# Grouped-query decode attention: the tokens of head 6's first values tile, ahead of GpSimd's last wait for the scaled output

## The chip, the core and the metric

One core of a Trainium2 chip runs the kernel. The metric is the device time of one execution in microseconds (us), lower is better. The engines are named as in the profile: PE is TensorE's matrix multiply, PEld its weight load, DVE is VectorE, ACT is ScalarE, POOL is GpSimd, SP is SyncE, which here only issues loads.

## What is computed

One decode step of attention: 32 query heads, one query each, over 8 key and value heads of 65,536 positions with 128 columns, all in bfloat16. Four query heads share one key and value head.

```python
k = jnp.repeat(k, rep, axis=1)          # rep = 32 // 8
v = jnp.repeat(v, rep, axis=1)
scores = jnp.einsum("bhqd,bhkd->bhqk", q, k) * D ** -0.5
p = softmax(scores, axis=-1)
return jnp.einsum("bhqk,bhkd->bhqd", p, v)
```

Keys and values are 268.4 MB together, and each byte is read once.

## The kernel before, in words

**Tiles and ring.** A head's keys and values are each two tiles of 256 rows by 128 partitions (64 KB on a partition, 8.4 MB in all). `buf` holds three of them. SP issues the 32 loads in the order of `tiles` (L153 to L156): from head 2 on `k g 0, k g 1, v g-2 1, v g-1 0`, and last `v 6 1, v 7 0, v 7 1`. Before it reuses a third of `buf`, SP waits until the tile in it has been used (L164, L169). I write v6.0 for the first values tile of head 6, and so on. The last tiles are loaded in pieces with a semaphore for each: v6.0 in 128 and 128 rows, v6.1 in 128, 64, 64, v7.0 in four of 64 (`BY`, L22, semaphores `sL`), and v7.1 in 64, 64, 32, 32, 40, 16 and 8 (`PIECES`, L27, semaphores `sP`).

**Tokens.** PE runs a loop of blocks, not a straight program. The block `values` (L481 to L494) takes one token from the semaphore `sV`, multiplies 32 rows of values by their weights `Ew` (8 matmuls, L486, into `psum_o`) and counts `vit` up by one. A tile of 256 rows is eight tokens. The tokens have no names: whoever counts `sV` up must do so in the order in which PE is to use the rows. For the tiles up to v5.1 SP hands out all eight once the tile has landed (L168). For v6.0 and what follows POOL does it, piece by piece (L216 to L218), `n // 32` tokens for n rows. The last 64 rows of v7.1 have no tokens; the block `tail` (L526) waits for their three pieces itself, the 40 rows at L532 to L538 (L535), the 16 and the 8 at L541 to L548 (L544).

**The round of a head.** PE computes scores of head g in four banks (`bank`, `scores`, L462), then v(g-2).1 in `values`, then `summed` (L502 to L515): it closes `psum_o` (L423), multiplies the maxima (L506), waits for DVE, clears `psum_o` (L420), gathers the result of head g-2 into `psum_f` (L433), and goes on to `values` for v(g-1).0. After that comes `turn` (L516), which takes one count of `wqs`. DVE works in parallel: it transposes the keys (L311) and the weights (L316), masks and sums `psum_o` (L324, L332), makes the maximum ready (L384) and the reciprocal (L338). ACT takes the exponential of the scores (L242), and then scales `psum_f` into `o_out` and counts `outs` up (L249).

**The end.** With the keys of head 7 scored, PE runs v5.1, `summed`, v6.0, `turn`, v6.1, `summed`, v7.0, `turn`, 192 rows of v7.1, and the tail with the last 64 rows, the sum (DVE L324, L332; PE L433), the last scaling (ACT L260) and the store.

**POOL's program around the change.** For g = 1 to 7 POOL waits until `outs` is g and writes the widened queries of head g (L204 to L213). Then it waits until `outs` is 8, counts `wqs` up by two for the two turns that are left (L214), and only then begins the loop that waits for each piece and hands out its tokens. `outs` becomes 8 when ACT has scaled head 5's output, behind the exponential of head 7.

Of the kernel before, what the change touches and what calls it, by code (L numbers as in the profile page):

```python
# [13 lines left out]
G = 8  # L14
# [3 lines left out]
NT = 256  # L18
# [3 lines left out]
BY = {  # L22
    (G - 2, 0): (128, 128), (G - 2, 1): (128, 64, 64), (G - 1, 0): (64, 64, 64, 64),
}
N = 2
STEP = 32
PIECES = (64, 64, 32, 32, 40, 16, 8)  # L27
MOVED = 4
# [3 lines left out]
def kernel(  # L32
# [24 lines left out]
    pe, dve, act, pool, sp = nc.tensor, nc.vector, nc.scalar, nc.gpsimd, nc.sync  # L57
# [38 lines left out]
    def sem(name):  # L96
        sems.append(nc.alloc_semaphore(name))
        return sems[-1]
# [3 lines left out]
    sL = [sem(f"sL{x}") for x in range(sum(map(len, BY.values())))]  # L102
    sP = [sem(f"sP{x}") for x in range(len(PIECES))]
# [5 lines left out]
    vit = sem("vit")  # L109
    scd = sem("scd")  # L110
    vdone = sem("vdone")
    wqs = sem("wqs")
# [7 lines left out]
    outs = sem("outs")  # L120
# [82 lines left out]
    for g in range(G):  # L203
# [7 lines left out]
            in1=quad[:, :].unsqueeze(1).unsqueeze(3).broadcast_to([P, 4, 4, H]),  # L211
            op=ALU.mult,
        ).then_inc(wqs, 1)  # L213
    pool.wait_ge(outs, G).then_inc(wqs, 2)  # L214

    for land, n in list(zip(sL, sum(BY.values(), ()))) + list(zip(sP, PIECES))[:MOVED]:  # L216

        pool.wait_ge(land, 32 if land is sP[0] else 16).then_inc(sV, n // STEP)  # L218

    def take(engine, semaphore, n=1):  # L220

        engine.wait_ge(semaphore, n).then_inc(semaphore, -n)  # L222
# [16 lines left out]
    for g in range(G + 1):  # L239
# [8 lines left out]
        at = max(g - 1, 0) * D  # L248
# [3 lines left out]
        if g == 0:  # L252

            for b in range(3):
                n = sum(kind == "k" and at % 3 == b and 0 < h < G - 1 for at, (kind, h, _) in enumerate(tiles))
# [200 lines left out]
    with block("scores"):  # L456
# [3 lines left out]
        for y in range(4 * N):  # L460
            m, n = y % 4, y // 4
# [64 lines left out]
    with block("tail"):  # L526
        at = sum(PIECES[:MOVED])
# [62 lines left out]
```

## Time and profile before

| what | value |
|---|---|
| runs | 631.0, 632.24, 632.6 us; median 632.24 |
| the profiled execution | 632.93 us |
| its span, first to last instruction | 630.7 us |
| bytes read, over the span | 268.44 MB, 426 GB/s |
| PE busy | 503.5 us, 80% of the span |
| DVE busy | 337.9 us, 54% |
| ACT and POOL busy | 21.1 us and 5.9 us |
| mean granted PE clock | 0.935 of full |

The profiled execution took 2.2 us more than its span; that is time outside the first and last instruction. All positions in time below count from the span's start. A row of the timeline gives the start, the length, engine, line and operation, and in brackets how long the engine had been idle and what ended it. A row of a window gives each engine's busy time in that stretch with its count of instructions, then the mean granted PE clock, the DMA engines' share (1.00 is all 16 busy; it can pass 1 in a short stretch, since a packet's time is put down whole) and the GB/s.

### The profile page before, as it was taken

The numbers are of one execution on the slowest core, as the hardware profiler recorded it, in microseconds if no ns is written. First come the engines' busy times: TensorE is split into PE (matmuls) and PEld (weight loads), VectorE is DVE, ScalarE is ACT, GpSimd is POOL, SyncE is SP. The second block draws the span as 40 slices with busy tenths as digits, with TensorE's granted clock in tenths as the row PEclk, the third lists the DMA queues.
The fourth block names the chain that finished last, engine by engine and source line by source line (L and its number), as shares of the span: only waits on it lengthen the run. The fifth ranks groups of instructions, "written<-read, shape, count | busy, mean of one in ns | idle before, by whom it ended". The sixth has DMA issues, their size and how long they took to land. (4 is left out here: it accounts for less than half of the span.)

```text
span 630.7 us, 8029 instructions
## 1 busy us (share of the span) xinstructions
PE 503.5 (80%) x2189; PEld 204.6 (32%) x2189; DVE 337.9 (54%) x118; ACT 21.1 (3%) x28; POOL 5.9 (1%) x16
## 2 busy tenths in 40 slices
PE   0685398898994979939799398994889987879998
PEld 0232043343331333314333133331333333323333
DVE  3984994789214882158721686217852688210100
ACT  1000100100010000100001000010000100010000
POOL 2000000000000000000000000000000000000000
PEclk9999599798998899988999798997999999898999
DMA  8999999999999999999999999999999999999995
GB/s 368 432 463 403 461 399 466 399 466 399 466 420 445 453 411 461 403 466 399 466 399 466 399 466 399 466 399 466 399 466 399 432 432 466 399 432 431 422 427 217
DMA packets 7000, 268.46 MB, mean 426 GB/s; under 512 B 856, under 2 KB 856, under 8 KB 1112
## 3 DMA queue, kind: packets, MB, share of 16 engines
q1 hardware_dynamic: 6912, 268.44, 98.8%
q10 hardware_dynamic: 88, 0.02, 0.0%
HBM read 268.44 MB, written 0.01 MB: 426 GB/s over the span
## 5 line engine op out<-in xcount | busy, mean ns | idle before, releaser
L311 DVE STREAM_TRANSPOSE buf<-buf 128x8192 f32<-128x8192 f32 x32 | 277.2, 8694 | 84.8 <-DVEq L222 84.8
L462 PE MATMUL sc<-buf,zeros 128*128 x1024 | 244.0, 396 | 0.0
L486 PE MATMUL psum_o<-buf,Ew 128*16 x1008 | 228.1, 385 | 13.6 <-PEq L222 9.7
L462 PEld LDWEIGHTS sc<-buf,zeros 128*128 x1024 | 101.6, 99 | 134.6 <-issue 38.7
L486 PEld LDWEIGHTS psum_o<-buf,Ew 128*16 x1008 | 90.2, 89 | 148.6 <-issue 55.1
L420 PE MATMUL sc<-zeros 128*128 128x512 bf16 x32 | 13.6, 426 | 87.2 <-PEq L222 87.0
L324 DVE TENSOR_TENSOR o_m<-psum_o,pick 128x512 f32<-128x512 f32 x10 | 7.0, 696 | 99.0 <-DVEq L222 72.1
L320 DVE COPY o_r<-o_r 4x1 f32<-4x1 f32 x9 | 1.3, 142 | 76.7 <-DVEq L222 64.1
L420 PEld LDWEIGHTS sc<-zeros 128*128 128x128 bf16 x32 | 3.1, 98 | 96.4 <-issue 95.4
L242 ACT ACTIVATE zeros<-sc,nmb 128x2048 bf16<-128x2048 f32 x8 | 15.7, 1967 | 536.6 <-DVE nmb L384 536.6
L316 DVE STREAM_TRANSPOSE Ew<-zeros 128x1024 bf16<-128x1024 bf16 x18 | 22.3, 1240 | 19.6 <-PE psum_o L486 19.5
L371 DVE TENSOR_REDUCE mx<-sc 128x1 f32<-128x2048 f32 x8 | 18.0, 2252 | 0.0
L506 PE MATMUL misc<-each,same 128*128 128x512 f32 x18 | 10.8, 685 | 8.3 <-PEq L222 8.3
L443 PE MATMUL misc<-qt,rep 32*128 32x128 bf16 x1 | 0.3, 281 | 10.6 <-DVE qt L301 10.6
L420 PE MATMUL psum_o<-zeros 128*128 128x512 bf16 x10 | 4.5, 446 | 5.3 <-PEq L222 5.3
L332 DVE TENSOR_REDUCE o_r<-o_m 128x128 f32<-128x512 f32 x10 | 6.9, 692 | 1.2
L208 POOL TENSOR_TENSOR zeros<-qx,quad 128x64 bf16<-128x64 bf16 x8 | 2.4, 294 | 487.6 <-ACT o_out L249 481.4
L506 PEld LDWEIGHTS misc<-each,same 128*128 128x128 f32 x18 | 2.9, 203 | 8.6 <-issue 8.5
L423 PE MATMUL sc<-zeros 128*128 128x1 bf16 x32 | 5.2, 163 | 0.0
L420 PEld LDWEIGHTS psum_o<-zeros 128*128 128x128 bf16 x10 | 1.0, 98 | 12.8 <-issue 12.6
L287 DVE CAST rep<-ident 32x128 bf16<-32x128 f32 x1 | 2.9, 2877 | 2.7 <-POOL ident L193 2.7
L423 PEld LDWEIGHTS sc<-zeros 128*128 128x128 bf16 x32 | 3.0, 95 | 3.9
(32 smaller groups left out, 37.3 us busy)
## 6 DMA issues: line engine op xcount, KB each, us to landing
buf<-in_k_dram SPq DMA_DIRECT2D x8, 4096.0 KB, 28.4
buf<-in_v_dram SPq DMA_DIRECT2D x8, 2048.0 KB, 34.4
buf<-in_v_dram SPq DMA_DIRECT2D x3, 4096.0 KB, 31.5
buf<-in_v_dram SPq DMA_DIRECT2D x2, 1024.0 KB, 32.7
buf<-in_v_dram SPq DMA_DIRECT2D x1, 1280.0 KB, 36.4
buf<-in_v_dram SPq DMA_DIRECT2D x1, 512.0 KB, 37.2
buf<-in_v_dram SPq DMA_DIRECT2D x1, 256.0 KB, 36.9
buf<-in_k_dram SPq DMA_DIRECT2D x12, 34.6
```

Source lines behind the costliest of these rows:

```text
L242: act.activation(out=E[:, :], in_=sc[:, :], func=ACT.Exp, bias=nmb[:, 0:1], scale=SCALE, accum_out=o_r[:, D:D + 1],).then_inc(exd, 1)
L287: dve.tensor_copy(out=rep[:, :].rearrange("p (a x) -> p a x", a=4), in_=ident[0:32, 0:32].unsqueeze(1).broadcast_to([32, 4, 32]),)
L311: dve.transpose(out=kv, in_=kv).then_inc(kt, 1)
L316: return dve.transpose(out=Ew[:, at], in_=E[:, at])
L324: return dve.tensor_tensor(out=o_m[:, :].rearrange("p (y d) -> p y d", y=4), in0=psum_o[:, :].rearrange("p (y d) -> p y d", y=4), in1=pick ...
L332: return dve.tensor_reduce(out=o_r[:, 0:D], in_=o_m[:, :].rearrange("p (y d) -> p d y", y=4), axis=AX.X, op=ALU.add)
L371: after(dve.tensor_reduce(out=mx[:, :], in_=sc[:, :], axis=AX.X, op=ALU.max))
L420: return pe.matmul(out=bank, lhsT=zer[:, 0:P], rhs=zer[:, :], start=True, stop=False)
L423: return pe.matmul(out=bank[:, 0:1], lhsT=zer[:, 0:P], rhs=zer[:, 0:1], start=False, stop=True)
L462: pe.matmul(out=bank, lhsT=moved(wq[:, m * SLIDE + 4 * n:][:, 0:P], slide), rhs=moved(T[:, n, m // 2, m % 2], keys), start=False, stop=False,)
L486: last = pe.matmul(out=psum_o[0:16, :], lhsT=moved(Ew[:, column(4 * j + 3):][:, 0:16], weight), rhs=moved(buf[:, 4 * j * D:][:, 0:4 * D], ...
L506: pe.matmul(out=misc[:, :], lhsT=same[:, :], rhs=each[:, :].unsqueeze(1).broadcast_to([P, 16, 32]), start=True, stop=True,).then_inc(pes, 1)
```

## The change

POOL's wait for `outs` at 8, with its two counts of `wqs`, moves from ahead of the loop into it: behind the second piece. In its old place stands a wait for `vit` at 96, that is for the last matmul of v5.1. So the two pieces of v6.0 are handed out, four tokens each, once v5.1 has been used and they have landed; then comes the wait for the scaled output, and then the pieces of v6.1, v7.0 and v7.1 as before.

```diff
-    pool.wait_ge(outs, G).then_inc(wqs, 2)
-
-    for land, n in list(zip(sL, sum(BY.values(), ()))) + list(zip(sP, PIECES))[:MOVED]:
+
+    pool.wait_ge(vit, NT // STEP * (2 * G - 4))
+    for at, (land, n) in enumerate(list(zip(sL, sum(BY.values(), ()))) + list(zip(sP, PIECES))[:MOVED]):
 
         pool.wait_ge(land, 32 if land is sP[0] else 16).then_inc(sV, n // STEP)
+        if at == 1:
+            pool.wait_ge(outs, G).then_inc(wqs, 2)
```

No other instruction changes on any engine.

## The prediction

> **What bounds the kernel now.** I read the DMA part of the page first: the loads on SP's queue kept the 16 DMA engines at work for 98.8% of the span.
>
> ```profile
> q1 hardware_dynamic: 6912, 268.44, 98.8%
> ```
>
> Then I cut the end of the span into stretches, and looked at the last two columns, DMA share and GB/s.
>
> ```profile
> 564.00:584.00 20.00, 16.91 (x66) 6.62 (x67) 0.46 (x4) 2.30 (x3) 0.00 (x0) 0.83 1.01 430
> 584.00:604.00 20.00, 19.30 (x87) 7.64 (x85) 3.77 (x6) 0.36 (x1) 0.00 (x0) 1.00 1.00 424
> 604.00:623.00 19.00, 17.99 (x83) 7.16 (x82) 0.00 (x0) 0.00 (x0) 0.00 (x0) 1.00 1.00 421
> 622.00:623.00 1.00, 1.00 (x6) 0.42 (x5) 0.00 (x0) 0.00 (x0) 0.00 (x0) 1.00 0.98 383
> 623.00:624.00 1.00, 1.00 (x7) 0.37 (x5) 0.00 (x0) 0.00 (x0) 0.00 (x0) 1.00 0.25 92
> 624.00:625.00 1.00, 1.00 (x6) 0.43 (x5) 0.00 (x0) 0.00 (x0) 0.00 (x0) 1.00 0.00 0
> ```
>
> The loads run without a gap (shares 1.01, 1.00, 1.00) and end about 623.25, a quarter into the stretch from 623. The span ends at 630.7. So the kernel is bound by its loads up to 623, and then 7.4 us follow in which nothing is loaded. Is that the unavoidable tail, or work that PE is behind with? PE's own timeline tells, from the end of v5.1 on:
>
> ```profile
> 561.21 0.18 PE L423 MATMUL psum_o<-zeros 128*128 128x1 bf16 x1
> 561.25 1.10 PE L506 MATMUL misc<-each,same 128*128 128x512 f32 x2
> 563.22 0.38 PE L420 MATMUL psum_o<-zeros 128*128 128x512 bf16 x1 [0.87 <-PEq L222]
> 563.52 0.38 PE L433 MATMUL psum_f<-o_r,sel 128*4 128x129 f32 x2
> 567.09 30.50 PE L486 MATMUL psum_o<-buf,Ew 128*16 x128 [3.19 <-POOLq L218]
> 597.52 0.18 PE L423 MATMUL psum_o<-zeros 128*128 128x1 bf16 x1
> 598.03 1.10 PE L506 MATMUL misc<-each,same 128*128 128x512 f32 x2 [0.33 <-PEq L222]
> 599.36 0.38 PE L420 MATMUL psum_o<-zeros 128*128 128x512 bf16 x1 [0.23 <-PEq L222]
> 599.66 0.38 PE L433 MATMUL psum_f<-o_r,sel 128*4 128x129 f32 x2
> 600.18 14.19 PE L486 MATMUL psum_o<-buf,Ew 128*16 x64
> 615.39 10.72 PE L486 MATMUL psum_o<-buf,Ew 128*16 x48 [1.01 <-PEq L222]
> 626.27 0.82 PE L535 MATMUL psum_o<-buf,Ew 128*16 128x512 bf16 x10 [0.17 <-issue]
> 627.02 0.18 PE L423 MATMUL psum_o<-zeros 128*128 128x1 bf16 x1
> 627.13 1.50 PE L544 MATMUL misc<-buf,Ew 128*4 128x128 bf16 x24
> 628.72 0.38 PE L433 MATMUL misc<-o_r,sel 128*4 128x128 f32 x2
> ```
>
> From 567.09 PE hardly rests: v6.0 and v6.1 in one row of 128 matmuls, v7.0 in 64, v7.1 in 48, then the tail. It is still at v7.1's first 192 rows at 626.11, three us after the last byte. To see that it wasn't waiting for those rows, I asked when POOL handed out tokens (its line 218 in five windows; "first to last", with the count):
>
> ```profile
> L218 POOLq EVENT_SEMAPHORE  x2: 17/17/17, 566.8 to 566.9; - x2
> L218 POOLq EVENT_SEMAPHORE  x3: 17/17/17, 574.8 to 584.6; - x3
> L218 POOLq EVENT_SEMAPHORE  x4: 17/17/17, 589.5 to 604.1; - x4
> L218 POOLq EVENT_SEMAPHORE  x2: 17/17/17, 609.0 to 613.9; - x2
> L218 POOLq EVENT_SEMAPHORE  x2: 17/17/17, 616.4 to 618.9; - x2
> ```
>
> All but the first row are landings: 64 rows every 4.9 us (574.8 to 584.6 is 128 rows, so 0.0766 us a row). The last token, for rows 160 to 191 of v7.1, is there at 618.9, and PE ends those rows 7.2 us later. **PE is the bound behind 567, running off a backlog.** The first row is the odd one: both tokens of v6.0 in one go, at 566.8, though by the spacing its pieces landed near 574.8 - 9.8 = 565.0 and 9.8 earlier, 555.2. What they waited for is ACT:
>
> ```profile
> 566.29 0.34 ACT L249 ACTIVATE o_out<-psum_f,o_r 4x128 bf16<-4x128 f32 x1
> ```
>
> It ends at 566.63, `outs` is 8, and POOL's wait is over.
>
> ```profile
> PE psum_o L486 <- POOLq L218: 3.2, 1, 3.2
> ```
>
> It is the only such wait of PE in the whole run.
>
> **The change, part by part.** *The pause.* With tokens there, PE goes from the gather (L433) to the values in 600.18 - 599.66 = 0.52 us, as it does for v7.0. For v6.0 that makes 563.52 + 0.52 = 564.04 instead of 567.09: 3.05 us. POOL's new wait is for v5.1's last matmul, before 561.25, so it and the first token, landed at 555.2, are 2.8 us early; the first four tokens are 32 matmuls, about 7 us, so the second piece (565.0) isn't waited for either.
>
> *The clock.* The column behind POOL's says what the pause did to PE:
>
> ```profile
> 565.00:566.00 1.00, 0.00 (x0) 0.00 (x0) 0.00 (x0) 1.00 (x1) 0.00 (x0) 0.89 1.21 524
> 566.00:567.00 1.00, 0.00 (x0) 0.00 (x0) 0.00 (x0) 0.63 (x3) 0.00 (x0) 0.50 1.22 524
> 572.00:573.00 1.00, 1.00 (x4) 0.33 (x3) 0.00 (x0) 0.00 (x0) 0.00 (x0) 0.69 1.07 459
> ```
>
> A mean of 0.89 over 565 to 566 is half clock from 565.78, and 0.69 over 572 to 573 is half clock until 572.62. So the first 5.5 us of v6.0 ran at half clock. The row of 128 matmuls took 30.50 us; two tiles at v7.0's pace would be 2 x 14.19 = 28.38. The slow start cost 2.12 us. Does it go with the pause? Here are stretches of 3.4 us around pauses:
>
> ```profile
> 531.70:535.10 3.40, 1.51 (x8) 0.57 (x6) 3.40 (x1) 0.00 (x0) 0.00 (x0) 1.00 0.71 308
> 541.90:545.30 3.40, 1.00 (x6) 0.35 (x4) 2.24 (x3) 0.00 (x0) 0.00 (x0) 1.00 1.07 463
> 562.40:565.80 3.40, 0.69 (x3) 0.19 (x3) 1.95 (x4) 1.47 (x1) 0.00 (x0) 1.00 1.08 463
> 565.80:569.20 3.40, 2.11 (x6) 0.75 (x7) 0.00 (x0) 0.83 (x3) 0.00 (x0) 0.50 0.78 337
> 597.20:600.60 3.40, 2.70 (x10) 0.83 (x9) 2.63 (x5) 0.16 (x1) 0.00 (x0) 1.00 1.08 458
> ```
>
> The clock halved behind those in which PE was busy for 1.00 and 0.69 us, and not behind those with 1.51 and 2.70. After the change PE is busy for 0.69 + (565.80 - 564.04) = 2.45 us of the third stretch, much like the fifth, which is the same round one head later. Wherever 3.4 us are laid over 561.2 to 564.04, more than 2 us are busy. I take the whole 2.12; the other end is none of it (rival B). PE's lead is then 3.05 + 2.12 = 5.17 us.
>
> [...]
>
> *What the lead is worth.* Step by step: v6.0 and v6.1 end at 564.04 + 28.38 = 592.42 (before: 597.59). The round takes 600.18 - 597.59 = 2.59, so v7.0 starts at 595.01 and ends at 609.20; its tokens come by 604.1, and its last 64 rows begin at 605.65. No wait. The turn takes 615.39 - 614.37 = 1.02, so v7.1 starts at 610.22, its first token at 609.0 being there. A matmul of v7.1 takes 10.72 / 48 = 0.223 us: 64 rows 3.57, 32 rows 1.79. The first 64 rows end at 613.79, and here PE meets the loads: the next token comes at 613.9, and with the 0.29 that PE took from 566.8 to 567.09 it goes on at 614.19. Then 617.76, 619.55 and 621.34, behind the tokens 616.4 and 618.9. The 40 rows of the tail land, at 0.0766 a row, at 618.9 + 3.06 = 621.96, the 16 at 623.2, the 8 at 623.8, which fits the end of the loads. So L535 starts at 622.25 and the close comes 0.75 later, at 623.00. From the close to the last gather were 628.72 - 627.02 = 1.70 us of DVE, which gives 624.70; but L544 takes 1.50 / 24 = 0.0625 a row, and starts its 16 rows at 623.2 + 0.29 = 623.5, ends them at 624.5 and the 8 at 625.0. The last gather moves from 628.72 to 625.0: **3.7 us**, and 1.4 of the lead goes into waits for landings.
>
> *Costs.* SP's seven loads of v7.1 wait for v6.0's end, so they are issued about 5.6 us before their present place:
>
> ```profile
> L134 SPq DMA_DIRECT2D buf<-in_v_dram x7: 328/432/4249, 583.8 to 587.0; - x7
> ```
>
> Behind them on SP stands only the wait for the end. They can't bring the loads' end forward: there is no gap to fill, and the issues already stand 22 us ahead of the first landing (587.0 to 609.0). On POOL, the counts for the turns stand behind the second piece (565.0) and `outs` (566.63), so they come at 566.8 as now; the first is needed at v6.0's end, 578.2, 11 us later. ACT and DVE start nothing earlier before 578. I take all of these at nothing.
>
> *The sum.* 632.93 for the profiled execution, less 3.7, is 629.2. That execution lies 0.7 above the median of the runs, 632.24. Part of that can be the slow clock, which ends in other places in other runs and on which the new end doesn't hang, part a general shift; I take half of it: **628.9 us**.
>
> **The rivals.**
>
> *B: the clock stays slow.* The half clock doesn't go with this pause, or the round's own gaps, 0.87 us and more, bring it too. Then only 3.05 us are won: v7.1 starts at 612.34, meets its tokens behind time (615.9 against 613.9), and the whole end moves by 3.05, to 629.9 for the profiled execution. For it: the clock fell 1.9 us into a pause, and 1.0 us busy was not enough elsewhere. Against it: the same round at 597 to 600 kept 1.00. [...]
>
> *C: the loads share.* The seven loads issued 5.6 us earlier could draw on the DMA engines beside v6.1 and v7.0 instead of behind them. At 578.2 some 84 rows of v6.1 are out (584.6 less 578.2, by 0.0766). Shared among three, they would take thrice 6.4 us, until 597.4, then v7.0 and v7.1 would come in together, and the last of v7.0 only about 623; PE would still have 64 of its rows (3.6), the turn (1.0) and v7.1's 192 rows (10.7) before L535, at 638.3 instead of 626.27: 645 us. The change loses as soon as v7.0's last token comes later than 614.37 - 3.55 = 610.8, now 604.1. Against it: today v7.1 is issued at 583.8 to 587.0 when the last rows of v6.1 and all of v7.0 are still out, and v7.0's tokens still come at the common spacing (589.5 to 604.1, 4.9 each).
>
> *D: it doesn't act.* The first tokens come no earlier than `outs`, because v6.0 lands later in other runs than here, or because v5.1's last count comes late. Then the time stays at 632.2. Against it: the first piece, by the spacing, is 11 us early.
>
> **How the numbers follow.** The forecast has a chance of 0.70, B (also a part of it) 0.15, D 0.09, C 0.06. The low end: if PE never waited, the end would be the last landing, 623.8 + 0.29 + 0.5 for 8 rows, a gather at 624.6 and 4.1 us won; with the full 0.7 below the profiled execution 628.1, and 0.4 for loads that differ between runs: 627.7. The high end is B's 629.9 with 0.6 for that: 630.5. Measurement can tell 0.3%, 1.9 us, so faster means below 630.3. Forecast and most of B are faster, 0.83; D and the edge of B the same, 0.11; C slower, 0.06.
>
> **What would show it.** PE's row L486 with 128 matmuls at 564.0 instead of 567.1, some 28.4 long, and no wait on POOL in front; the clock at 1.00 in 565 to 573; tokens from 574.8 on unmoved; short waits for tokens inside v7.1; loads ending at 623 and the last gather about 625. If the loads end later, or a token of v7.0 does, C is at work and the forecast is wrong; a row of 30.5 at 564.0 is B.

## The result, and the profile after

The changed kernel takes 628.88 us (median of 4 runs, 628.31 to 629.08), the kernel before 632.42 in the same comparison (4 runs, 631.0 to 633.18). The ratio is 0.9945, 95% interval 0.9926 to 0.9964: 3.5 us faster. In the first set of experiments it took 628.85 (0.9949, 0.9936 to 0.9962).

PE's timeline of the changed kernel from v6.0 on (start, length, engine, line, operation, count, idle time before and what ended it; the change adds two lines, so L486 is now L488, L535 is L537, L544 is L546):

```profile
562.57 14.19 PE L488 MATMUL psum_o<-buf,Ew 128*16 x64
577.81 14.22 PE L488 MATMUL psum_o<-buf,Ew 128*16 x64 [1.05 <-PEq L224]
...
594.71 14.19 PE L488 MATMUL psum_o<-buf,Ew 128*16 x64
609.91 3.71 PE L488 MATMUL psum_o<-buf,Ew 128*16 x16 [1.01 <-PEq L224]
613.84 7.14 PE L488 MATMUL psum_o<-buf,Ew 128*16 x32 [0.21 <-PEq L224]
621.61 0.82 PE L537 MATMUL psum_o<-buf,Ew 128*16 128x512 bf16 x10 [0.64 <-DMA buf<-in_v_dram]
622.36 0.18 PE L425 MATMUL psum_o<-zeros 128*128 128x1 bf16 x1
622.90 1.50 PE L546 MATMUL misc<-buf,Ew 128*4 128x128 bf16 x24 [0.36 <-DMA buf<-in_v_dram]
624.24 0.38 PE L435 MATMUL misc<-o_r,sel 128*4 128x128 f32 x2
```

The pause of 3.19 us in front of v6.0 is gone. New are short waits at the end: 0.21 for v7.1's second token, 0.64 for the 40 rows, 0.36 for the 16, and the last two name a load. The row of 128 matmuls has become two of 64 with 1.05 us between them; that is the turn, and it comes up again below. The tokens that POOL hands out (line 218, by the same five windows):

```profile
L218 POOLq EVENT_SEMAPHORE  x1: 17/17/17, 564.6 to 564.6; - x1
L218 POOLq EVENT_SEMAPHORE  x3: 17/17/17, 574.4 to 584.1; - x3
L218 POOLq EVENT_SEMAPHORE  x4: 17/17/17, 589.0 to 603.9; - x4
L218 POOLq EVENT_SEMAPHORE  x2: 17/17/17, 608.6 to 613.5; - x2
L218 POOLq EVENT_SEMAPHORE  x2: 17/17/17, 616.0 to 618.5; - x2
```

The first piece's tokens, ahead of these windows, are handed out at 559.8, when v5.1 ends. From 574 on the tokens come as before, 0.2 to 0.5 us earlier. That lead isn't the change's: in the second profile of the changed kernel (the first experiment) they come from 574.8 to 619.0, against 574.8 to 618.9 before. The clock and the loads, in stretches of the changed kernel (the last three columns are clock, DMA share, GB/s):

```profile
564.00:584.00 20.00, 18.95 (x88) 7.46 (x86) 1.25 (x1) 1.20 (x3) 0.00 (x0) 1.00 0.99 423
584.00:604.00 20.00, 19.28 (x86) 7.42 (x85) 2.63 (x5) 0.36 (x1) 0.00 (x0) 1.00 1.01 430
622.00:623.00 1.00, 0.64 (x10) 0.20 (x4) 0.43 (x1) 0.00 (x0) 0.00 (x0) 1.00 0.83 313
623.00:624.00 1.00, 1.00 (x20) 1.00 (x19) 0.96 (x2) 0.00 (x0) 0.00 (x0) 1.00 0.00 0
```

The clock is full where it was 0.83 on average, and the loads end at 622.8 instead of 623.25. The page's chain that ended last now has the load of v7.1 in it, which in the kernel before it had not:

```profile
DMA 6%; PE 3%; SPq 1%; issue 0%; ACT 0%
```

One thing in this profile is not the change: v5.1, ahead of it, ran quicker. The first row is of the kernel before, the second of the changed one.

```profile
545.95 15.33 PE L486 MATMUL psum_o<-buf,Ew 128*16 x64 [3.05 <-PEq L222]
```

```profile
545.53 14.23 PE L488 MATMUL psum_o<-buf,Ew 128*16 x64 [3.05 <-PEq L224]
```

Behind the same pause of 3.05 us the clock halved in one execution (0.50 from 546 to 548) and not in the other (1.00). So I count PE's lead from the end of v5.1 (L423 at 561.21 before, L425 at 559.78 after). From there to the end of v6.1 (597.52; 592.05 after) it is 36.31 us before and 32.27 after: **4.04 us**.

### The profile page after: what moved, and what is told of

The parts are those of the page before. It is cut to its first block, busy times and chain, and to the rows that moved or that the text cites. A ratio compares the mean times of both kernels' runs of the same rounds, so it can differ in the third digit from the quotient of the medians.

```text
span 626.2 us, 8029 instructions
## 1 busy us (share of the span) xinstructions
PE 501.6 (80%) x2189; PEld 203.4 (32%) x2189; DVE 337.8 (54%) x118; ACT 21.1 (3%) x28; POOL 5.9 (1%) x16
## 5 line engine op out<-in xcount | busy, mean ns | idle before, releaser
L488 PE MATMUL psum_o<-buf,Ew 128*16 x1008 | 224.6, 380 | 11.8 <-PEq L224 10.9
L488 PEld LDWEIGHTS psum_o<-buf,Ew 128*16 x1008 | 88.6, 88 | 144.7 <-issue 55.8
L425 PE MATMUL sc<-zeros 128*128 128x1 bf16 x32 | 5.2, 163 | 0.0
L425 PEld LDWEIGHTS sc<-zeros 128*128 128x128 bf16 x32 | 3.0, 95 | 3.9
```

Of the source, the lines that this page charges most:

```text
L425: return pe.matmul(out=bank[:, 0:1], lhsT=zer[:, 0:P], rhs=zer[:, 0:1], start=False, stop=True)
L488: last = pe.matmul(out=psum_o[0:16, :], lhsT=moved(Ew[:, column(4 * j + 3):][:, 0:16], weight), rhs=moved(buf[:, 4 * j * D:][:, 0:4 * D], ...
```

## The experiments

Two theories stood at the start. **L**: the loads set the end now, and PE waits for landings. **P**: PE still sets the end, and the gain is PE's lead, whatever it is.

**The changed kernel again**, beside the next three.

> The changed kernel itself, beside the kernel before and the other kernels of this set. Theory L (PE no longer bounds the end; v7.1's landings do, and PE waits for them): 628.5 to 629.3 us, PE waiting for landings inside v7.1 and ahead of the 40 rows, loads ending 3.3 us before the span does. Theory P (the end still moves with PE one to one, and the gain is PE's lead and no more): the same time, but no waits for landings in the trace.

628.85 us (628.52 to 629.11). PE waited 0.52 us for the 40 rows and 0.35 for the 16, as L has it, but not inside v7.1.

**Five matmuls on zeros ahead of v6.0**, in the round of head 7 only: the block `summed` branches there to a block of its own.

```diff
+        pe.br_eq(g, G, on_true="busy", on_false="go_on")
+    with block("go_on"):
         pe.br_ne(g, 1, on_true="values", on_false="turn")
...
+    with block("busy"):
+        for _ in range(5):
+            pe.matmul(
+                out=psum_o[:, :], lhsT=zer[:, 0:P], rhs=zer[:, :], start=False, stop=False
+            )
+        pe.br("values")
```

> Five matmuls on zeros, added to psum_o in the round of head 7 alone, between the gather and v6.0: PE starts v6.0 later by 5 x 0.215 = 1.07 us. PE waited for landings for 0.21 + 0.64 us in v7.1 and its tail. Theory L: part of the delay is taken up by those waits, 629.1 to 629.5 us, 0.2 to 0.6 above the changed kernel. Theory P: 1.07 above it, 630.0 us.

629.11 us (628.46 to 629.59; ratio to before 0.9952, 0.994 to 0.9964): 0.26 above the changed kernel, of 1.07 put in. That lies in L's range, but it doesn't part L from P. In its profile the zeros put PE back by only 0.42 us, not 1.07 (v7.1 starts 50.55 us behind the end of v5.1, against 50.13 in the changed kernel), so P too would have given 629.27; the next shows why. Nor did PE wait for a landing there: v5.1 had started at half clock (0.50 from 546 to 548, 15.33 us), and 0.17 us of idle time, not put down to a load, stood ahead of the 40 rows.

**Fourteen of them.**

> Fourteen such matmuls: v6.0 starts 14 x 0.215 = 3.0 us later, where the kernel before starts it, but PE has been busy in the pause. It parts the pause from the clock. Theory L with the clock (the slow start costs time of its own): v6.0 runs at full clock, two tiles take 28.4 and the turn 1.05, so the end is 2.2 to 3.0 us above the changed kernel and below the kernel before by the slow start, 1.0 us or more: 631.0 to 631.5. Rival N (the clock cost nothing, the pause is all): as the kernel before, 632.4 us.

629.86 us (628.73 to 630.62; 0.996, 0.9946 to 0.9973). That is 1.0 above the changed kernel and 2.4 below the kernel before, and lower than I expected under either theory. Its v6.0 starts nearly as late behind the end of v5.1 as in the kernel before (5.76 us against 5.88), but look at how long the two tiles take:

```profile
564.36 3.19 PE L532 MATMUL psum_o<-zeros 128*128 128x512 bf16 x14
567.49 27.79 PE L488 MATMUL psum_o<-buf,Ew 128*16 x128
```

27.79 against 30.50 before and 14.19 + 1.05 + 14.22 = 29.46 in the changed kernel. At first I read the 2.71 as the price of the slow clock. But the changed kernel had a full clock too and was 1.67 slower. With five matmuls the rows lie between:

```profile
564.87 13.98 PE L488 MATMUL psum_o<-buf,Ew 128*16 x64
579.36 14.22 PE L488 MATMUL psum_o<-buf,Ew 128*16 x64 [0.51 <-PEq L224]
```

The turn's gap is 1.05 with none, 0.51 with five, and none to be seen with fourteen. So I put two readings against each other: K, the clock is the price, and W, something else comes with work queued in front.

**The kernel before, with its wait in place, and twelve matmuls on zeros in the pause.** The same branch and block in the kernel before, with `range(12)`.

> The kernel before, with GpSimd's wait where it was, and twelve matmuls on zeros (2.6 us) in the pause ahead of v6.0. Only the clock is changed, not the time at which v6.0's tokens come (566.8). With fourteen of them and the wait moved, v6.0 started at 567.5 and the two tiles took 27.8 us instead of 30.5. Theory K (the slow clock behind the pause is the larger part of the gain): v6.0 at 567.1, two tiles in 27.8, the end 2.3 to 2.7 us below the kernel before: 629.5 to 629.9. Rival W (the wait is the larger part, and fourteen matmuls gained by the moved wait): 631 us or more.

631.5 us (12 runs, 630.64 to 633.92) against 631.91 for the kernel before; 0.9993, 0.9979 to 1.0006. No difference that this can tell, and the interval's end, 1.3 us below, rules out the 2.3 to 2.7 of K: K falls, and W's 631 or more is met. The trace says why.

```profile
565.15 2.76 PE L530 MATMUL psum_o<-zeros 128*128 128x512 bf16 x12
568.40 14.20 PE L486 MATMUL psum_o<-buf,Ew 128*16 x64 [0.49 <-POOLq L218]
583.65 14.22 PE L486 MATMUL psum_o<-buf,Ew 128*16 x64 [1.05 <-PEq L222]
```

```profile
568.40:597.80 29.40, 28.34 (x128) 11.21 (x128) 1.25 (x1) 0.00 (x0) 0.00 (x0) 1.00 1.00 427
```

PE was kept busy, the clock was full (1.00, the third column from the right), and still the two tiles took 14.20 + 1.05 + 14.22 = 29.47. The difference to the fourteen is the tokens. There the first had been handed out when v5.1 ended, before PE came to the zeros; here they came at 568.1, when the zeros were done. So the slow clock alone cost 30.50 - 29.47 = **1.03 us** net by the rows' lengths. The other 1.68, of which 1.05 is the turn and the rest, 0.63, lies within the two tiles (14.20 + 14.22 against 27.79), go with PE's sequencer (PEq), which takes the tokens and works through the loop's turn: can it do so while matmuls are still running? Its records show when it took the first token of v6.1, in the changed kernel, the one with fourteen, and the kernel before:

```profile
L224 PEldq EVENT_SEMAPHORE  x1: 51/51/51, 577.5 to 577.5; - x1
```

```profile
L224 PEldq EVENT_SEMAPHORE  x1: 51/51/51, 579.8 to 579.8; - x1
```

```profile
L222 PEldq EVENT_SEMAPHORE  x1: 51/51/51, 582.0 to 582.0; - x1
```

In the changed kernel v6.0's matmuls had ended at 576.76, so PE stood idle. In the other two PE came to the first matmul of v6.1 some 1.5 us after that token (583.6 in the timeline of before; with fourteen 581.3, an estimate: the end of the row, 595.28, less the 13.98 of v6.0 with five), and no gap shows. That also explains why the kernel before showed one unbroken row of 128: behind the stretch at half clock the sequencer was ahead (582.0, 583.6), and the turn was hidden.

**Less work for PE behind v5.1.** Of the eight matmuls in a run of the `values` block the last is left out, in the changed kernel and in the kernel before. The block serves all tiles, so PE is also earlier ahead of v6.0: in the kernel before v5.1 ends at 558.60 instead of 561.21.

```diff
-        for j in range(STEP // 4):
+        for j in range(STEP // 4 - 1):
```

> The changed kernel, leaving out the last of the eight matmuls in each run of the values block (the last 4 of every 32 rows of values). From v6.0 on PE has 3 x 8 + 6 = 30 matmuls less, 30 x 0.215 = 6.4 us. Theory L (the landings of v7.1 set the end): PE only waits longer, the end comes with the last landing: 628.2 to 628.9, at most 0.6 below the changed kernel. Theory P (PE sets the end): 628.85 - 6.4 = 622.4.

> The kernel before with the same matmuls left out: the pause and the slow clock are still there, but PE has 6.4 us less to do behind them, more than the 3.4 us by which it was late. Theory L: the end falls onto the same landings, 628.3 to 629.0, as the changed kernel and as the changed kernel with these matmuls left out. Theory P: 632.24 - 6.4 = 625.8, and 3.4 above the changed kernel with the same left out.

628.59 us (628.35 to 628.8; 0.994, 0.9927 to 0.9953) and 628.77 (628.53 to 629.09; 0.9945, 0.9931 to 0.9958). The expected cut of 6.4 us gave the changed kernel 0.26, and it brought the kernel before, pause and slow clock included, to the same end as the change does. P is out by 6 us and by 3. The rows of v7.0 and v7.1 in the kernel before with less work:

```profile
564.48 26.88 PE L486 MATMUL psum_o<-buf,Ew 128*16 x112 [3.18 <-PEq L222]
...
594.11 9.68 PE L486 MATMUL psum_o<-buf,Ew 128*16 x42
604.12 3.27 PE L486 MATMUL psum_o<-buf,Ew 128*16 x14 [0.34 <-PEq L222]
609.03 3.31 PE L486 MATMUL psum_o<-buf,Ew 128*16 x14 [1.64 <-PEq L222]
613.91 6.63 PE L486 MATMUL psum_o<-buf,Ew 128*16 x28 [1.58 <-PEq L222]
621.67 0.82 PE L535 MATMUL psum_o<-buf,Ew 128*16 128x512 bf16 x10 [1.13 <-DMA buf<-in_v_dram]
```

It still has the pause (3.18), but waits for each token from 604 on, and begins the 40 rows at 621.67, where the changed kernel began them at 621.61. **With less work for PE the end is the landings**, and the changed kernel comes within 0.26 us of that. The pause cost time only because PE had no spare time behind it to make it up.

**Only the first piece handed out early**: `if at == 0` instead of `if at == 1`.

> Only the first piece of v6.0, 128 rows, is handed out ahead of the wait for the scaled output. Those four blocks keep PE busy for 7 us from 564, and the wait is over at 566.2 to 566.8, so the second piece needs no lead: 628.9, as the changed kernel. If the lead of the second piece mattered: 0.3 or more above it.

628.97 us (628.41 to 629.2; 0.9943, 0.9928 to 0.9958). The second piece needs no lead, as expected.

**The wait too late**: `if at == 4`, behind v6.1's pieces.

> The wait for the scaled output stands three pieces later, behind all of v6.1 instead of behind v6.0. The first of the two counts for the turns then comes at v6.1's last landing, 584.1, and not at 565. If PE's turn between v6.0 and v6.1 takes it as the code reads, PE stands from 577 to 584.4 with a halved clock behind that: v6.1 until about 600, v7.0 603 to 617, v7.1 618 to 629, the end about 633.5 of span, 635 us or more, slower than before by 0.4%. If the place of that wait behind the first tile doesn't matter: 628.9 us.

636.31 us (636.22 to 636.33; 1.0066, 1.0051 to 1.0081), slower than before by 4.1.

```profile
565.41 14.19 PE L488 MATMUL psum_o<-buf,Ew 128*16 x64
585.57 15.76 PE L488 MATMUL psum_o<-buf,Ew 128*16 x64 [5.97 <-PEq L224]
```

PE stands at the turn from 579.60 until POOL has got past the landing of v6.1's last piece: its wait for `outs` is over at 584.5, and PE goes on at 585.57. So the place of the wait has two edges: ahead of the first piece it holds v6.0, behind the second tile's pieces it holds the turn.

**A finer cut of the tail**: `PIECES = (64, 64, 32, 32, 36, 12, 8, 8)`.

> The changed kernel with v7.1's last 64 rows in pieces of 36, 12, 8 and 8 instead of 40, 16 and 8. Theory L: the end hangs on the last landings alone, so a better cut of them moves it: the 36 rows land 0.3 us earlier and with them the masking and summing, and the rows behind are worked off as they land, ending 0.5 us after the last landing instead of 0.9: 628.5, 0.35 below the changed kernel. Theory P: 628.85, no change, or later by the extra wait.

628.96 us (628.25 to 630.28; 0.9948, 0.9934 to 0.9963): no gain, L's 0.35 missed. In its profile v5.1 had started at half clock (0.50 from 547 to 549) and taken 15.66 us, and PE came to the 36 rows with no load to wait for:

```profile
611.38 10.72 PE L488 MATMUL psum_o<-buf,Ew 128*16 x48 [1.01 <-PEq L224]
622.26 0.81 PE L537 MATMUL psum_o<-buf,Ew 128*16 128x512 bf16 x9 [0.17 <-issue]
```

The one-piece kernel's profile looks the same (v5.1 15.66 us, 0.17 in front of the 40 rows). There PE began the 40 rows 3.7 us behind the last token (622.72, 619.0), and in the changed kernel's two profiles, where it waited for them, 3.1 us behind (621.61, 618.5; 622.09, 619.0). So in these profiles L holds where v5.1 ran at full clock, with less than one us to spare. Where v5.1 started slow, PE came to these rows about 0.6 us late and set the end again.

**The clock held up ahead of v5.1**: eight matmuls on zeros behind head 7's scores, in the changed kernel, without and with the finer cut.

```diff
-        pe.br_lt(g, 2, on_true="summed", on_false="values")
+        pe.br_lt(g, 2, on_true="summed", on_false="of_last")
+    with block("of_last"):
+        pe.br_eq(g, G - 1, on_true="busy", on_false="values")
```

The block `busy` is as above, with `range(8)`.

> The changed kernel with eight matmuls on zeros between the scores of head 7 and v5.1, in the pause of 2 to 3 us there, behind which some profiles show a halved clock and others don't. Theory V (whether v5.1 starts slow decides whether PE still meets the landings; that is what is left of PE in the end): no halved clock in 540 to 570, waits for landings in v7.1 or its tail, 628.6 us and at most 0.5 between the runs. Rival: 628.9 as the changed kernel, with runs as far apart as its own, 0.6.

> The same eight matmuls, with v7.1's last rows cut in 36, 12, 8 and 8. With the cut alone PE had no wait for landings left in the profile (v5.1 had started slow), and nothing was won. Theory V: with PE early, the cut's 0.35 us show: 628.2 to 628.4. Rival (the cut has no worth by itself, its extra load costs what it wins): 628.6 to 629.0.

628.51 us (628.39 to 628.95; 0.9939, 0.9927 to 0.9951) and 628.29 (628.24 to 628.69; 0.9934, 0.9922 to 0.9946). The second is the best of all: five of its six runs lie between 628.24 and 628.34, and of the changed kernel's nine runs one does (628.31), the others being 628.52 to 629.11. It is 0.6 us of 629 below the change, which the intervals of the two ratios don't part, and the kernel before was 0.3 lower too in this set (631.91; 632.24 in the first); the cut's 0.2 between these two lies within the spread of their runs. In both profiles the clock is 1.00 from 540 to 573, and the waits for landings are back, as V has it (without the cut 0.28 inside v7.1, 0.61 ahead of the 40 rows and 0.36 ahead of the 16; its runs spread over 0.56, a little more than the 0.5 expected). With the finer cut:

```profile
543.49 1.90 PE L532 MATMUL psum_o<-zeros 128*128 128x512 bf16 x8 [0.29 <-issue]
546.21 14.20 PE L490 MATMUL psum_o<-buf,Ew 128*16 x64 [0.82 <-PEq L224]
...
614.62 7.14 PE L490 MATMUL psum_o<-buf,Ew 128*16 x32 [0.37 <-PEq L224]
622.08 0.81 PE L546 MATMUL psum_o<-buf,Ew 128*16 128x512 bf16 x9 [0.32 <-DMA buf<-in_v_dram]
```

## Why the prediction was right, and where a term was off

*What bounds.* Right: behind 567 PE was the bound, and with less work for PE the kernel before ends where the changed one does (628.77 against 628.85).

*The pause.* Forecast 3.05 us, v6.0 2.83 us behind the end of v5.1. Measured 562.57 - 559.78 = 2.79 against 567.09 - 561.21 = 5.88: 3.09. POOL's new wait, the counts for the turns and SP's earlier issues cost nothing that shows.

*The clock.* The step was right in kind, and the term was mis-sized. The half clock did go with the pause: in the changed kernel's profile the clock is 1.00 from 564 to 584, and v6.0 took 14.19 us in the one-piece and the finer-cut kernels too, so rival B is out. But I priced it at 30.50 less two tiles of 14.19, which gave 2.12, and forgot the turn between the tiles. The row of 128 had hidden it, and it comes back as 1.05 us once PE runs at full clock. By the rows' lengths the term is 1.04 (30.50 - 29.46), and the kernel before with its pause filled gave the same, 1.03. Counted from the start of v6.0 to the close behind v6.1 it is 0.95 (30.43 before, 29.48 after), since in the timeline the row of before ends at 597.59, 0.07 behind the start of the close, and the changed kernel's at 592.03, 0.02 ahead of it. The stretches of 3.4 us by which I judged the pauses were my choice, and no run shows that the busy time in them decides: in the changed kernel's profile PE was busy for 0.59 us from 541.90 to 545.30, less than in any of the five, and the clock stayed at 1.00 behind it. With the 3.09 that makes the lead of 4.04 us, and not 5.17.

*What the lead is worth.* Right in kind: in the changed kernel's two profiles the landings cap it. I had 1.4 of the 5.17 going into waits and 3.7 left. With the true 4.04, and v5.1 as in the profile of before, PE would come to the 40 rows at 622.24 (61.03 us behind the end of v5.1, as in the one-piece kernel's profile), and they are there at 622.0, 3.1 us behind the last token of 618.9. The end would be PE's by a little, and nothing of the lead would go into waits. The times worked out ahead at which PE goes on with the 40 and the 16 rows (622.25 and 623.5) fit: the second profile of the changed kernel, with its last token at 619.0, has 622.09 and 623.37. That 628.9 stands beside 628.88 is in part luck: the error of 1.1 us in the lead fell into the 1.4 that the forecast gave to waits, and the half of the 0.7 in the sum was a choice. A lead one us smaller would have made the error in the clock's term visible.

*The median.* I took half of the 0.7 us between the profiled execution and the median as the clock falling elsewhere. The spreads fit that: in the first comparison, with four runs each, the kernel before spread over 2.2 us (631.0 to 633.18) and the changed one over 0.8 (628.31 to 629.08). That the clock behind v5.1's pause is the reason is not shown: only the profiled executions tell of it.

*The rivals.* C, that the loads would share: v7.1's loads were issued from 576.8 instead of 583.8, and the tokens of v6.1 and v7.0 came 4.9 us apart as before. D, that it would not act: PE went from the gather to v6.0 without a wait (562.57).

## What to carry to other kernels

When a kernel waits for memory most of the time, look for the stretch in which it does not: here the last 60 us, in which an engine 80% busy over the whole span had no time left to make up a pause of 3 us. Before you price an engine's lead, work out when the data lands that it is to run on, since the landings can cap the gain and hide an error in the lead, as here one of 1.1 us. And where an engine's later work stands behind a wait, as POOL's tokens do here, move the wait only past what it isn't needed for: three pieces further the same line cost 7.5 us.

## What the runs showed of the hardware that was not expected

PE's sequencer was ahead of the matmuls in some of these profiles and behind them in others: the same 128 matmuls at full clock took 29.46 us where it took the next tile's first token 0.8 us behind the last matmul of v6.0 (577.5, 576.76), and 27.79 with 14 matmuls queued in front, where it took it 1.5 us ahead of the first of v6.1 (579.8, 581.3). Behind the half-clock stretch of the kernel before it was 1.6 us ahead too (582.0, 583.6) and no gap shows at the turn, so the net cost of that stretch, about 1 us, was less than half of the 2.7 us that its matmuls lost against the unbroken row (30.50, 27.79). In the kernel before with less work it cost nothing: at a clock of 0.50 from 565 to 568 it took 27.01 us from the start of v6.0 to the close behind v6.1, and the changed kernel with less work, at full clock, 27.00.

The same pause ahead of v5.1, 3.05 us, left the clock full in the changed kernel's profile (v5.1 in 14.23 us), and halved it in the kernel before (15.33) and in the kernel before with twelve matmuls (16.90, at a clock of 0.50 from 545 to 551):

```profile
545.69 16.90 PE L486 MATMUL psum_o<-buf,Ew 128*16 x64 [3.05 <-PEq L222]
```

With eight matmuls on zeros in that pause it took 14.20 both times, at a clock of 1.00. Both ways occur behind 3.05 us (14.23 and 16.90 us), so the length of the pause alone doesn't decide; what does, no run here shows.
